# Delta-rule attention feeding a gated MLP: products of zeros that wait for the solve's steps, another order of the first chunk, weights held back, and the two correction products taken head by head

## The chip, the cores and the metric

The kernel runs on one core of a Trainium2 chip. The metric is the device time of one execution in microseconds (us), compared as the median of several executions.

## What is computed

```python
def _attn_ref(q, k, v, beta):                    # 4 x 8 heads, 768 steps, head size 48
    k_n = k / (np.linalg.norm(k, axis=-1, keepdims=True) + 1e-06)
    for t in range(S):
        kt, vt, bt = (k_n[:, :, t], v[:, :, t], beta[:, :, t, None])
        y[:, :, t] = np.einsum('bhd,bhde->bhe', q[:, :, t], state)
        v_old = np.einsum('bhde,bhd->bhe', state, kt)
        state = state + bt[:, :, :, None] * np.einsum('bhd,bhe->bhde', kt, vt - v_old)
...
def _moe_ref(x, w_in, w_out):                    # x is 3072 x 384, hidden 2048
    h = x @ w_in
    sp = np.where(h > 20.0, h, np.log1p(np.exp(np.minimum(h, 20.0))))
    g = h * np.tanh(sp)
    return (g @ w_out).astype(np.float32)
```

The attention's output, with its heads side by side, is the input x of the MLP. The weights arrive as 64-bit numbers.

## The kernel before

**Chunks.** The 768 steps are cut into 12 chunks of 64. Within a chunk the recurrence is a triangular system. Its matrix comes from the Gram products of the keys (`pg`), is solved on VectorE in a chain of short steps (`pr`, `gt`, lines 605 and 606), and is turned into a matrix T (`tt`) and its transpose (`tn`). Two chunks are solved together: group 0 is chunks 0 and 1, group 1 is chunks 2 and 3. A diagonal block has 32 rows. Groups 0 and 1 solve blocks of 16 rows and join them by two sets of small products, `ma` and `mb` (lines 650 and 661). Then the two 32-row blocks of a chunk are joined by two products for each pair of heads, `ta` (function `s_a`) and `tb` (`s_b`). After that come, for each half of the heads, `gq` (queries and state against keys), `pz` (Z~, the corrected values), `py` (the output) and `ps` (the new state), and `xt`, which turns the output into x.

**The MLP.** For each chunk `moe` runs 8 blocks of hidden units: 18 products `h` (line 960), the activation `e` and its split `g`, and 12 products `acc` (line 970). The product is made in two halves of precision, so each weight is split too.

**The weights.** They come in 28 parts, 12 of `w_in` (`ri`, 512 KB) and 16 of `w_out` (`ro`, 384 KB). `convert` takes each from 64-bit words to a high and a low half: a scaled copy on ScalarE, a clamp and a sign on GpSimd or VectorE, two joins on VectorE (line 399), and for the parts in `LO_PE` the low half by products on TensorE (`loi`, `loo`, lines 416 and 418). A part below number `FIRST` is issued without waiting for the one ahead of it; the others wait until the one ahead has landed, and from `FREE` on only every second one waits.

**The order.** All loads of weights, keys and values stand in SyncE's queue, in order. A planner (`Plan.run`) plays all operations through with assumed durations and priorities, and writes each engine's instructions down in the order that this gives. It also keeps count of TensorE's instructions: 448 are taken to be there at the start, and further ones come in packets of 256. Tiles in PSUM are rings: four of tag `ps`, so `gq` of chunk 0, which writes four, holds all of them until the masks of line 838 have read them. `warm` is products of zeros into a tile that nobody reads.

The first chunk's TensorE work has negative priorities, written by hand at the end of the kernel:

```python
    for h in range(2):
        turn_q(0, h, -90.4 + 0.1 * h, q0)
        issue(-89.5 + 0.1 * h, s_gq(0, h))
    issue(-90, s_a(0))
    issue(-89, s_b(0))
```

## Time and profile before

| | us |
|---|---|
| median of 3 executions (lowest, highest) | 646.77 (645.03, 647.28) |
| the profiled execution | 645.29 |
| span of its instructions | 643.4 |
| TensorE busy | 602.8 |
| VectorE busy | 452.3 |
| ScalarE busy | 277.8 |
| GpSimd busy | 143.2 |

The span runs from the first to the last instruction; 1.9 us of the execution lie around it. PE is TensorE's products, PEld its weight loads, DVE VectorE, ACT ScalarE, POOL GpSimd, SP SyncE and SPq its DMA queue. PEclk is the granted TensorE clock as a share of full speed: 1.00 is 2.4 GHz, 0.50 is 1.2 GHz. In the trace one 32-bit product is recorded as two MATMULs and two LDWEIGHTS, so `x32` is 16 products of the code.

### The profile page before, as it was taken

To read this page: it belongs to the slowest core of one execution; us is meant where nothing else is said; L and a number is where in the kernel's file an instruction comes from. 1 tells how busy PE (TensorE), PEld (TensorE's weight loads), DVE (VectorE), ACT (ScalarE), POOL (GpSimd) and SP (SyncE) were. 2 spreads that over 40 slices of the span, in tenths; PEclk is the share of its full clock that TensorE was granted. 3 is DMA by queue.
4 is the path that set the end of the run, shared out by engine and by line. 5 is a ranking of instruction groups with operands and counts; after the bars stand their busy time and mean duration, and the time that the engine had idled before them with its cause. 6 is when DMAs were issued, how large, how long until landed. Compare 5 with 4: busy or idle time off the path is not lost.

```text
span 643.4 us, 20696 instructions
## 1 busy us (share of the span) xinstructions
PE 602.8 (94%) x8928; PEld 558.7 (87%) x8928; DVE 452.3 (70%) x964; ACT 277.8 (43%) x601; POOL 143.2 (22%) x146
## 2 busy tenths in 40 slices
PE   7339998995999999999999999999999999999997
PEld 7126677895999999999999999999999999999997
DVE  2866887899366999578999578997689994622110
ACT  2515888540554332544333644225543336343331
POOL 5646789241103110103111004001031101000000
PEclk8856996997899999999999999999999999999999
DMA  7764775210324110442112252104141111110011
GB/s 109 233 163 102 206 183 128 51 25 2 53 39 65 38 32 9 74 64 39 40 38 47 34 90 41 30 16 70 19 64 38 39 37 15 26 27 1 1 25 25
DMA packets 156251, 37.61 MB, mean 58 GB/s; under 512 B 149504, under 2 KB 152576, under 8 KB 156160
## 3 DMA queue, kind: packets, MB, share of 16 engines
q1 hardware_dynamic: 151040, 35.80, 28.0%
q8 instruction: 70, 1.15, 0.7%
q10 hardware_dynamic: 5120, 0.49, 0.6%
q14 instruction: 21, 0.17, 0.1%
HBM read 31.56 MB, written 4.72 MB: 56 GB/s over the span
## 4 chain that ended last, share of the span: by engine, by line
PE 69%; DVE 18%; DMA 5%; issue 3%; SPq 2%; POOL 1%; ACT 1%; DVEq 0%; ACTq 0%; POOLq 0%
PE acc L970 26%; PE h L960 25%; DVE pr L605 4%; DVE gt L606 3%; PE py L680 3%; DMA ri<-in_moe_w_in_dram 2%; PE gq L680 2%; PE tb L680 2%; PE pz L680 2%; DVE g L977 2%; DMA ksrc<-in_k_dram 2%; SPq L301 2%; PE pg L483 1%; PE ta L680 1%; PE ps L680 1%
## 5 line engine op out<-in xcount | busy, mean ns | idle before, releaser
L970 PE MATMUL acc<-wo,g 128*128 128x384 f32 x1152 | 225.7, 345 | 0.5 <-DVE g L977 0.5
L960 PE MATMUL h<-x,wi 128*128 128x256 f32 x1728 | 224.1, 284 | 0.0
L960 PEld LDWEIGHTS h<-x,wi 128*128 128x128 f32 x1728 | 213.4, 188 | 4.6 <-DVE x L939 0.7
L970 PEld LDWEIGHTS acc<-wo,g 128*128 128x128 f32 x1152 | 201.1, 191 | 4.2 <-DVE g L977 1.7
L977 DVE TENSOR_TENSOR g<-e,g 128x512 fp32r<-128x512 f32 x96 | 71.9, 753 | 103.9 <-ACT g L976 103.4
L975 ACT ACTIVATE e<-h 128x512 f32<-128x512 f32 x96 | 57.4, 598 | 162.6 <-DVE g L977 89.1
L976 ACT CAST g<-e 128x512 fp32r<-128x512 f32 x96 | 59.5, 619 | 61.9 <-PE acc L970 60.6
L512 POOL TENSOR_TENSOR d<-at,lmask 32x512 f32<-32x512 f32 x20 | 27.0, 1351 | 130.3 <-DVE d L498 94.1
L606 DVE TENSOR_TENSOR gt<-gt,pr 128x84 f32<-128x84 f32 (+14 forms) x148 | 51.9, 351 | 5.1
L605 DVE TENSOR_TENSOR pr<-gt 128x84 f32<-128x84 f32 (+14 forms) x148 | 52.3, 353 | 3.8
L838 DVE TENSOR_TENSOR xx<-gq,amask 64x256 f32<-64x256 f32 x96 | 40.5, 422 | 2.0
L638 POOL COPY tt<-tt 32x512 f32<-32x512 f32 x24 | 17.1, 714 | 100.2 <-DVE tt L621 85.2
L783 POOL TENSOR_TENSOR vt<-vt,ne 128x384 f32<-128x384 f32 x22 | 20.1, 932 | 72.4 <-DMA vt<-in_v_dram 67.5
L831 DVE TENSOR_TENSOR vt<-vt,gq 64x192 f32<-64x192 f32 (+1 forms) x66 | 23.2, 352 | 15.9 <-PE gq L680 11.4
L699 ACT COPY xx<-pz 64x192 f32<-64x192 f32 x92 | 28.9, 314 | 11.4 <-PE pz L680 10.1
L904 DVE TENSOR_TENSOR xx<-xx,ps 48x192 f32<-48x192 f32 x80 | 28.2, 352 | 3.2 <-PE ps L680 1.8
L680 PE MATMUL gq<-xx,kt 64*64 64x112 f32 (+1 forms) x768 | 30.0, 261 | 0.0
L680 PEld LDWEIGHTS py<-xx 128*64 128x64 f32 x768 | 24.3, 138 | 6.1 <-issue 3.7
L791 DVE STREAM_TRANSPOSE xx<-qsrc 64x512 f32<-64x512 f32 x40 | 28.2, 706 | 1.2
L650 PE MATMUL ma<-tu,d 16*32 16x16 f32 x512 | 7.2, 202 | 22.8 <-DVE xx L838 15.4
L680 PE MATMUL pz<-vt,tt 64*64 64x48 f32 x768 | 27.6, 225 | 0.8 <-ACT tt L699 0.8
L650 PEld LDWEIGHTS ma<-tu,d 16*32 16x32 f32 x512 | 6.8, 139 | 24.1 <-issue 23.5
(143 smaller groups left out, 690.9 us busy)
## 6 DMA issues: line engine op xcount, KB each, us to landing
ri<-in_moe_w_in_dram SPq DMA_DIRECT2D x12, 512.0 KB, 4.6
ro<-in_moe_w_out_dram SPq DMA_DIRECT2D x16, 384.0 KB, 4.3
vt<-in_v_dram SPq DMA_DIRECT2D x24, 192.0 KB, 3.5
xx<-in_k_dram SPq DMA_DIRECT2D x48, 96.0 KB, 2.9
out_dram<-o SPq DMA_DIRECT2D x48, 96.0 KB, 2.2
ksrc<-in_k_dram SPq DMA_DIRECT2D x44, 64.0 KB, 2.6
qsrc<-in_q_dram SPq DMA_DIRECT2D x40, 64.0 KB, 2.5
ksrc<-in_k_dram SPq DMA_DIRECT2D x44, 32.0 KB, 2.5
```

Source lines behind the costliest of these rows:

```text
L605: nc.vector.tensor_tensor(out=pv, in0=nj, in1=xj, op=ALU.mult)
L606: nc.vector.tensor_tensor(out=below, in0=below, in1=pv, op=ALU.add)
L680: nc.tensor.matmul(*a, start=True, stop=True)
L699: (nc.scalar.copy if e == "ACT" else nc.vector.tensor_copy)(out=a, in_=b)
L791: nc.vector.transpose(xx[h][r, :, hh, D:D + C], src)
L838: nc.vector.tensor_tensor(out=x[r, p4, hh, D:D + C], in0=pg[h4]()[i, :, d:], in1=bcast_mid(amask[i], 4), op=ALU.mult)
L904: nc.vector.tensor_tensor(out=old, in0=old, in1=ps[h4]()[i], op=ALU.add)
L960: nc.tensor.matmul(h()[:, f2, :], wt["i", f * P // WI * NCH + c][:, i2, f0:f0 + P], x[:, c, :], start=(i == 0), stop=(i == 3 * NCH - 1))
L970: nc.tensor.matmul(acc[t]()[:, :DM], gg()[:, a, f2, ts_], wt["o", f][:, i2, :], start=(f == 0 and i == 0), stop=(f == NF - 1 and i == 2))
L975: m = op("ACT", 0.58, prio + 0.1, lambda e=e, h=h: nc.scalar.activation(e(), h(), AF.Mish, scale=-1.0), m, bufs=[h, e])
L976: m = op("ACT", 0.58, prio + 0.1, lambda e=e, gg=gg: nc.scalar.copy(out=gg()[:, 0], in_=e()), m, bufs=[e, gg])
L977: m = op("DVE", 0.7, prio + 0.1, lambda e=e, gg=gg: nc.vector.tensor_tensor(out=gg()[:, 1], in0=e(), in1=gg()[:, 0], op=ALU.subtract), m, ...
```

## The change

It has five parts. (1) The products of zeros at the start are 15 of 512 columns in place of 66 small ones. Those beside the solve no longer follow each other freely: `warm_after` puts four behind a step of the solve, and three behind the last join of the first ten weight parts, with a semaphore wait on that very instruction; the planner leaves out a group that it would place over 0.5 us after the step. (2) Both Grams of group 0 come ahead of the turning of the queries (`grams[1]` in `qread`), the queries' load waits for the first Gram, the values' load for the queries', and by the planner's order `gq` of chunk 0 now stands behind `mb`. (3) Nine weight parts instead of six are issued without waiting (`FIRST`), and the tenth waits for the product Z~ of chunk 0's first half of heads (`GATE`); those behind it are loaded one at a time up to the 26th (`FREE`). (4) From chunk 2 on `ta` and `tb` are products of one head, 32x32 each, over four places of the array; chunks 0 and 1 keep the old form as `s_a2` and `s_b2`. (5) The planner's model of instruction packets is different, small products next to each other get a slight preference (`TOGETHER`), four priorities move, the 25th part's low half goes to TensorE, and `py` of chunk 0 no longer waits for the keys that only `ps` reads.

```diff
-    THERE, PACKET, ASK, TAKES = 448, 256, 308, 2.6
+    THERE, PACKET, ASK, AHEAD, TAKES = 448, 256, 244, 64, 2.6
+    CHANGE, TOGETHER = 0.2, 0.0
...
-                    times = [(max(free[e], when(o)), o.prio, i, o) for i, o in enumerate(ops)]
+                    times = [(max(free[e], when(o)), o.prio - self.TOGETHER * (group and o.words >= 64), i, o)
+                             for i, o in enumerate(ops)]
...
+            if o.late is not None and t > o.after[0].free + o.late:
+                o.took, o.words, o.bufs, o.fn = 0.0, 0, [], lambda: None
...
+            if n == 0 and hh == 0:
+                tc.add_manual_dep(d.ins, gram_ins[0].name, SYNC, reason="instructions first")
...
-    def load_w(kind, i, paced):
+    def load_w(kind, i, paced, gate):
...
+        if gate:
+            tc.add_manual_dep(d.ins, marks[gate].name, SYNC, reason="instructions first")
...
+        if k < WARM:
+            warm_after(o, 3)
...
-            for i in range(few + n):
-                m = 32 if i < few else P
-                nc.tensor.matmul(warm()[0:m, 0:4 * m], zero()[:, 0:m], zero()[:, 0:4 * m], start=True, stop=True)
+            for i in range(n):
+                x = identr.bitcast(BF16) if after in marks else zero()[:, 0:512]
+                p = nc.tensor.matmul(warm()[:, :x.shape[1]], x[:, 0:P], x, start=True, stop=True)
+                if i == 0 and after in marks:
+                    tc.add_manual_dep(p.ins, marks[after].name, SYNC, reason="not before")
...
-    WARM = {2: 2, 8: 12}
-    keep_warm(0, o, -210, few=66)
+    marks, WARM = {}, 10
+    def warm_after(o, n):
+        f = o.fn
+        def marked():
+            marks[o] = f()
+        o.fn = marked
+        keep_warm(n, o, -85)
+    keep_warm(15, o, -210)
...
-            if g == 0 and j in WARM:
-                keep_warm(WARM[j], o, -96)
+            if g == 0 and j > 1:
+                warm_after(o, 4)
...
+    def halves():
+        return [PB * i + p for p in range(PB) for i in range(2)]
...
+    def s_a(n):
+        at, tt = ats[n], tt2[:, n % 2]
+        ps = buf("ps", [P, NP, 32], f"ta{n}")
+        def products():
+            for p in halves():
+                for hh in range(2):
+                    r = slice(64 * hh + 32, 64 * hh + 64)
+                    i = 64 * hh + 32 * (p // PB)
+                    yield ps()[i:i + 32, p, :], at()[r, p, :], tt[r, p, 32:]
...
+    def s_b(n):
...
+            for p in halves():
+                for hh in range(2):
+                    r = slice(64 * hh, 64 * hh + 32)
+                    i = 64 * hh + 32 * (p // PB)
+                    yield ps()[i:i + 32, p, :], tn()[r, n % 2, p, :], at()[r, p, :]
...
-        m = qread[n, h] = op("PE", 1.0, prio, products, *got, eyer, ydn.get((n - 1, h)), gdn.get((n - 1, h)), bufs=[ps], words=64)
+        m = qread[n, h] = op("PE", 1.0, prio, products, *got, eyer, grams[1], ydn.get((n - 1, h)), gdn.get((n - 1, h)), bufs=[ps], words=64)
...
-                     [*zdn[n, h], *ptr[n, h], *kxd[n, h], cleared_rest, *(() if y else (ydn[n, h],))],
+                     [*zdn[n, h], *ptr[n, h], *(kxd[n, h] if state else ()), cleared_rest, *(() if y else (ydn[n, h],))],
...
-    E1S, LAG, PRIO_XT, CV0, CV1, G1A, XA, GQ2 = 0.471, 3, 0.289, -0.48, 0.819, 1.125, 0.027, 0.985
-    LO_PE = range(24)
-    FIRST, FREE = 6, 13
+    E1S, LAG, PRIO_XT, CV0, CV1, G1A, XA, GQ2 = 0.471, 3, 0.354, -0.48, 0.919, 1.108, 0.027, 0.985
+    LO_PE = range(25)
+    FIRST, FREE = 9, 26
+    plan.TOGETHER = 0.019
+    GATE = 3
...
-    q0, v0 = load_q(0, -99.5), load_v(0, -99.4)
+    q0 = load_q(0, -99.5, grams[0])
+    last_s["v"] = q0
+    v0 = load_v(0, -99.4)
...
+    first = [issue(-90, s_a2(0)), issue(-89, s_b2(0))]
+    first += [issue(-88 + 0.1 * h, s_z(0, h)) for h in range(2)]
+    first += [issue(-87 + 0.1 * h, s_y(0, h, state=False)) for h in range(2)]
+    if GATE:
+        stop[0] = first[GATE - 1]
+        got[FIRST].after.append(stop[0])
```

Where the instructions go is shown at three places. The first is TensorE from the end of chunk 0's Gram to chunk 0's Z~, of the kernel before; `kt_194` and `kt_277` are the turned keys of chunks 0 and 1, and each line of one kind stands once for its run.

```order
L489 MATMUL pg_1_205<-kt_194 32x64 x4
L804 MATMUL qt_0_290<-identr,qsrc 48x64 x16
L804 MATMUL qt_1_307<-identr,qsrc 48x64 x16
L489 MATMUL pg_0_326<-kt_277 32x64 x4
L446 MATMUL warm<-zero 128x512
L680 MATMUL gq_00_477<-xx_80,kt_194 64x64 x2
L650 MATMUL ma_591<-tu_576,d_266 32x16 x64
L661 MATMUL mb_665<-tt_82,ym_281 32x16 x64
L416 MATMUL loi_743<-mi_429,identr 128x512
L680 MATMUL ta_748<-tt_82,at_267 64x64 x16
L418 MATMUL loi_743<-wi_745,identr 128x512
L680 MATMUL tb_775<-at_267,tn_733 64x64 x16
```

The same stretch of TensorE after the change, where `kt_223` is chunk 1's keys.

```order
L523 MATMUL pg_0_232<-kt_223 32x64 x4
L895 MATMUL qt_0_318<-identr,qsrc 48x64 x16
L895 MATMUL qt_1_339<-identr,qsrc 48x64 x16
L465 MATMUL warm<-identr 128x256
L684 MATMUL ma_496<-tu_491,d_214 32x16 x64
L695 MATMUL mb_571<-tt_82,ym_227 32x16 x64
L717 MATMUL gq_00_644<-xx_80,kt_143 64x64 x2
L717 MATMUL ta_666<-tt_82,at_215 64x64 x16
L436 MATMUL loi_686<-mi_384,identr 128x512
L717 MATMUL gq_10_692<-xx_81,kt_143 64x64 x2
L438 MATMUL loi_686<-wi_569,identr 128x512
L717 MATMUL tb_719<-at_215,tn_642 64x64 x16
```

Chunk 1's Gram now follows chunk 0's at once; `gq` has gone from ahead of `ma` to behind `mb`, its two halves on either side of `ta`; between the queries' turning and `ma` stand 16 products of zeros (four behind each of the steps 2 to 5 of the solve), and none behind the steps 6 to 14.

The second place is SyncE's queue from the first weight parts on. Before:

```order
L348 DMA ro_420<-in_moe_w_out_dram 128x768
L348 DMA ro_498<-in_moe_w_out_dram 128x768
L301 DMA xx_80<-in_k_dram 64x8x48 x2
L348 DMA ri_560<-in_moe_w_in_dram 128x1024
L301 DMA xx_81<-in_k_dram 64x8x48 x2
L348 DMA ri_582<-in_moe_w_in_dram 128x1024
L301 DMA vt_584<-in_v_dram 64x16x48 x2
L348 DMA ri_659<-in_moe_w_in_dram 128x1024
```

And after the change, where `ri_784` is the tenth part, the one that waits for Z~:

```order
L363 DMA ro_374<-in_moe_w_out_dram 128x768
L363 DMA ri_377<-in_moe_w_in_dram 128x1024
L363 DMA ri_380<-in_moe_w_in_dram 128x1024
L312 DMA qsrc<-in_q_dram 64x16x48 x2
L363 DMA ri_784<-in_moe_w_in_dram 128x1024
L312 DMA xx_80<-in_k_dram 64x8x48 x2
L363 DMA ro_848<-in_moe_w_out_dram 128x768
L312 DMA xx_81<-in_k_dram 64x8x48 x2
```

The eighth and ninth part moved ahead of the wait; chunk 0's keys for the state (`xx_80`, `xx_81`) and all that stands behind moved behind it.

The third place is TensorE in the steady part, `ta` and `tb` of chunks 2 and 3, whose middle ones are issued four and four. Before:

```order
L680 MATMUL ta_2560<-tt_82,at_1869 64x64 x16
L680 MATMUL tb_2604<-at_1869,tn_2485 64x64 x4
L680 MATMUL ta_2605<-tt_82,at_1907 64x64 x4
L680 MATMUL tb_2794<-at_1907,tn_2485 64x64 x16
```

And after:

```order
L717 MATMUL ta_2551<-tt_82,at_1863 32x32 x32
L717 MATMUL tb_2627<-at_1863,tn_2452 32x32 x4
L717 MATMUL ta_2628<-tt_82,at_1902 32x32 x4
L717 MATMUL tb_2846<-at_1902,tn_2452 32x32 x32
```

Each has twice as many products of half as many columns.

## Rows read from the trace of the kernel before

**Rows 1.** Busy time of each engine by stage, from the windows of the trace: start and end, length, then for PE, PEld, DVE, ACT and POOL busy us (instructions), then the granted clock, the share of the DMA engines and GB/s.

```profile
37.00:69.50 32.50, 25.35 (x510) 17.72 (x511) 21.30 (x41) 14.95 (x33) 16.70 (x12) 0.64 0.56 133
69.50:136.30 66.80, 64.39 (x1052) 52.73 (x1052) 56.15 (x98) 49.41 (x107) 47.45 (x34) 0.92 0.52 126
180.00:643.00 463.00, 458.62 (x6082) 438.67 (x6074) 323.40 (x704) 186.32 (x401) 48.44 (x52) 1.00 0.22 38
```

**Rows 2.** The same view cut where the granted clock changes (the column before the last two).

```profile
26.00:37.00 11.00, 0.00 (x0) 0.00 (x1) 10.16 (x26) 4.73 (x14) 9.63 (x7) 0.50 0.58 148
37.00:60.00 23.00, 16.75 (x392) 11.72 (x392) 12.01 (x25) 7.18 (x16) 13.43 (x10) 0.50 0.43 108
60.00:97.50 37.50, 35.65 (x611) 26.17 (x610) 32.78 (x55) 32.02 (x69) 26.36 (x19) 1.00 0.80 201
```

**Rows 3.** The timeline of the first 21 us: start, length, engine, line, operation, out<-in, count, and in brackets the idle time ahead with what ended it.

```profile
7.06 2.05 PE L489 MATMUL pg<-kt 64*32 64x64 f32 x128
8.18 1.25 DVE L467 STREAM_TRANSPOSE kt<-ksrc 128x1024 f32<-128x1024 f32 x1 [1.40 <-DMA ksrc<-in_k_dram]
...
11.55 2.95 PE L804 MATMUL qt<-identr,qsrc 64*48 64x64 f32 x62 [1.72 <-DMA qsrc<-in_q_dram]
...
14.43 2.60 PE L489 MATMUL pg<-kt 64*32 64x64 f32 x128
...
17.50 1.39 PE L680 MATMUL gq<-xx,kt 64*64 64x64 f32 x64
...
18.82 2.76 PE L446 MATMUL warm<-zero 128*128 128x512 bf16 x12
```

**Rows 4.** The timeline from the end of the solve to Z~ and to the first `h`, same columns.

```profile
33.33 1.07 DVE L619 STREAM_TRANSPOSE tu<-gt 128x512 f32<-128x512 f32 x1
...
36.05 3.48 DVE L838 TENSOR_TENSOR xx<-gq,amask 64x256 f32<-64x256 f32 x8
37.03 2.10 PE L650 MATMUL ma<-tu,d 16*32 16x16 f32 x128 [15.44 <-DVE xx L838]
...
43.15 1.78 PE L661 MATMUL mb<-tt,ym 32*32 32x16 f32 x115 [3.15 <-issue]
...
46.76 2.07 PE L416 MATMUL loi<-mi,identr 128*128 128x512 f32 x2 [1.83 <-DVE mi L399]
...
48.76 1.97 PE L680 MATMUL ta<-tt,at 32*64 32x64 f32 x32
...
50.66 0.80 PE L418 MATMUL loi<-wi,identr 128*128 128x512 f32 x1
...
53.09 1.97 PE L680 MATMUL tb<-at,tn 32*64 32x64 f32 x32
...
56.56 2.34 PE L680 MATMUL pz<-vt,tt 64*64 64x48 f32 x64 [0.77 <-ACT tt L699]
...
69.55 2.65 PE L960 MATMUL h<-x,wi 128*128 128x256 f32 x21
```

**Rows 5.** The profile's page: busy time and instructions of TensorE, and the queue that carries instructions (packets, MB, share of 16 engines); then, from its list of loads, the queries' load of chunks 0 and 1 (count, KB, us from issue to landing).

```profile
PE 602.8 (94%) x8928; PEld 558.7 (87%) x8928; DVE 452.3 (70%) x964; ACT 277.8 (43%) x601; POOL 143.2 (22%) x146
...
q8 instruction: 70, 1.15, 0.7%
...
qsrc<-in_q_dram SPq DMA_DIRECT2D x4, 192.0 KB, 3.5
```

**Rows 6.** The timeline of SyncE's queue, weight parts alone: from one row to the next is the interval of paced loads.

```profile
35.45 0.33 SPq L348 DMA_DIRECT2D ri<-in_moe_w_in_dram  x1
...
39.77 0.33 SPq L348 DMA_DIRECT2D ri<-in_moe_w_in_dram  x1
...
44.03 3.44 SPq L348 DMA_DIRECT2D ro<-in_moe_w_out_dram  x2
...
95.17 0.83 SPq L348 DMA_DIRECT2D ro<-in_moe_w_out_dram  x2
...
100.43 0.82 SPq L348 DMA_DIRECT2D ro<-in_moe_w_out_dram  x2
```

**Rows 7.** The timeline around the start of the second solve (line 526 turns its matrix).

```profile
126.34 0.56 DVE L399 SCALAR_TENSOR_TENSOR solved<-solved,ro 128x384 int32<-128x384 int32 x1 [1.10 <-POOL ro L392]
...
128.73 2.38 PE L960 MATMUL h<-x,wi 128*128 128x256 f32 x18
...
130.06 5.77 POOL L512 TENSOR_TENSOR d<-at,lmask 32x512 f32<-32x512 f32 x4 [3.75 <-ACT at L503]
...
136.30 2.06 DVE L526 STREAM_TRANSPOSE gt<-d 128x1024 f32<-128x1024 f32 x1
```

**Rows 8.** The timeline of small products at full clock: `mb` of chunk 1, and the first row of the `tb` and `ta` that are issued four and four, with the first row behind them.

```profile
94.27 1.26 PE L661 MATMUL mb<-tt,ym 32*32 32x16 f32 x128
...
267.21 0.27 PE L680 MATMUL tb<-at,tn 32*64 32x64 f32 x2
...
268.35 2.40 PE L960 MATMUL h<-x,wi 128*128 128x256 f32 x18
```

**Rows 9.** The chain of work that ended last, near the same place: start, us, what.

```profile
259.65 2.11 PE acc L970 x12
...
263.89 1.08 PE ta L680 x32
264.97 2.31 PE acc L970 x12
```

More of the change, by code (lines that the diff above doesn't have):

```diff
@@ L29, in __init__ @@
         self.bufs = bufs
-        self.next, self.left, self.free, self.kb, self.words, self.sync = [], 0, None, 0, 0, False
+        self.next, self.left, self.free, self.kb, self.words, self.sync, self.late = [], 0, None, 0, 0, False, None
 class Buf:
@@ L80, in feed @@
                 there, done = there + self.PACKET, None
-            if done is None and there <= self.ASK and left > 0:
+            if done is None and there <= self.ASK + min(self.AHEAD, left + 32) and left > 0:
                 done = t + self.TAKES + max(0.0, line - t)
@@ L95, in run @@
     def run(self):
-        there, due = self.THERE, None
+        there, due, group = self.THERE, None, False
         free, line, used, ready, flying = {}, 0.0, {}, {}, []
@@ L149, in run @@
                     used.setdefault(b.tag, []).append(b)
+            if o.words:
+                if group and o.words >= 64 and t < free[e] + 0.1:
+                    o.took -= self.CHANGE
+                group = o.words >= 64
             free[e] = t + o.took
@@ L679, in run_all @@
                 for a in f[i:i + 4]:
-                    nc.tensor.matmul(*a, start=True, stop=True)
+                    last = nc.tensor.matmul(*a, start=True, stop=True)
+        return last.ins
     class Stage:
@@ L688, in issue @@
     def issue(prio, *stages):
-        m = op("PE", sum(s.took for s in stages), prio, lambda: run_all(*(s.products() for s in stages)),
+        def products():
+            marks[m] = run_all(*(s.products() for s in stages))
+        m = op("PE", sum(s.took for s in stages), prio, products,
                *(a for s in stages for a in s.after), bufs=[b for s in stages for b in s.bufs], words=sum(s.words for s in stages))
```

63 lines of the change are left out of this document (43 added, 20 removed).

## The prediction

> **What bounds the kernel now.** I read the windows by stage first. From 180 us to the end TensorE is busy 458.6 of 463 us at full clock [rows 1]: that stretch ends sooner only if TensorE has less to do. The room lies ahead of it. Between 26 and 60 us the clock is 0.50, which is 1.2 GHz, and in the first 11 us of that TensorE does nothing [rows 2]; up to 136 us it is busy nearly throughout, with VectorE at 56.2 of 66.8 us [rows 1]. So I read the start as a chain in the timeline, link by link.
>
> Four waits stand in it. (a) Chunk 1's keys are turned at 9.43 us (8.18 + 1.25), but its Gram starts at 14.43, because the queries' turning stands ahead of it in TensorE's queue and waits for a load until 11.55 [rows 3]. (b) The solve's result `tu` is there at 34.40, but `ma` starts at 37.03. The four PSUM tiles are held by `gq` until the masks have read the first, and those are VectorE's next work, from 36.05 on [rows 4]. (c) `mb` stops after 13 recorded products for 3.15 us, with nothing that the profile can name [rows 4]. TensorE's 8928 products and 8928 loads over the 70 packets of the instruction queue make 255 a packet [rows 5]. Counted in the order, 1210 instructions lie ahead of the stop (products of zeros 132 + 4 + 24, Grams 2 x 256, turning 128, `gq` 128, `ma` 256, `mb` 26), and the plan's own constants make 448 + 3 x 256 = 1216. So I take it for a missing packet. (d) Chunk 0's stage from `ma` to `pz` runs at half clock [rows 2, 4].
>
> Then the weights: once `h` has begun at 69.55 [rows 4], the next fixed point is the second solve, whose matrix is turned at 136.30. Ahead of it, in VectorE's order, stands the join of the last weight part at 126.34; GpSimd's four products `d` end at 135.83 [rows 7].
>
> **The change, part by part.**
>
> *Grams first.* Chunk 1's Gram can start at 9.45 instead of 14.43: -5.0. What follows keeps its order. The queries' load is now issued after the first Gram's end at 9.11 [rows 3]; with 3.5 us to landing [rows 5] the queries are there at about 12.6, and ScalarE's copy of them, which stands ahead of the solve's root, ends as the root is wanted. If the load lands 2 us later, 2 us go: the bounds are -3.0 and -5.0.
>
> *`gq` behind `mb`.* No tile is held at `ma`: it starts 0.1 us after `tu`, -2.5. The masks move to VectorE's wait for `mb`, so they cost nothing until `ta`'s result wants VectorE.
>
> *The packet.* Up to `ma` there are now 30 + 256 + 256 + 128 + 32 = 702 instructions, and `ma` has 256. The boundary 960 falls at the head of `mb` again, but no weight load is under way then, where before a 512 KB part was issued at 39.77, inside the stop [rows 6]. I take -3.0; the bounds are 0 and -3.15.
>
> *Between `mb` and `tb`.* This takes 8.15 us now, from 44.94 to 53.09. Afterwards a half of `gq` (0.7 at full, 1.4 at half clock), `ta` (1.90), a `loi` (2.07), the other half, 0.72 and another `loi` (1.7) stand in a row: 9.2 at half clock, +1.0, or 4.9 at full, -3.2 [rows 3, 4]. The products of zeros don't decide it. They end behind step 5 of the solve, at about 22 us, some 7.5 us ahead of `ma`; in the trace the clock fell at 26.0, 4.4 us after the last such product at 21.58 [rows 2, 3]. So `ma` starts at half clock again. Afterwards TensorE has fewer gaps than now and may rise earlier. Between the ends I take 0.
>
> *From `tb` to `h`.* Six products of zeros stand ahead of `xt`, and each group waits for a join that VectorE does just then. They are 128x256, half of the 0.23 us that a 512-column one took [rows 3]: +0.3, with bounds 0 and +0.7. The 15 at the very start lie in TensorE's wait for the keys and cost nothing.
>
> Together: -5.0 - 2.5 - 3.0 + 0 + 0.3 = -10.2. `h` starts at 59.3, and the first half of Z~, now at about 57.7, ends at 47.2.
>
> *Weights held.* Seventeen parts go one at a time from 47.2 us on, then a pair. Alone, a 512 KB part took 4.3 us and a 384 KB part 3.1 (39.77 to 44.03, and the second of the next row); in the thick of the other loads a pair took 5.3 (95.17 to 100.43) [rows 6]. Seven large and ten small ones make 3.6 on average alone; 5.3 is the other end, if one costs what a pair costs. A pair also moves a second part, so I take 4.0, nearer to the lone rows. Then the 26th has landed at 115 and the last pair at 120.5, some 15 us later than now. With 3.5 us for copy, clamp and sign the last join stands at 124, only 2.3 us sooner than 126.34. Behind it come `d`, the copies and two of GpSimd's products (2.9 of the 5.77), so the matrix is turned at about 130.3 instead of 136.30 [rows 7]. TensorE gives the same: from `h` to the seventh `h` it takes 59.2 us now [rows 4, 7], one `acc` (2.2) comes ahead, a part's low half and three groups of zeros add 2.2, and 59.3 + 63.6 = 122.9 is 5.8 sooner. So 4.2 of the 10.2 are given back. The bounds are 0 and, at 5.3, far more than all of it (below).
>
> The second solve and the wait for it keep their length. What stands behind them on TensorE is the same `h` and `acc`.
>
> *Single heads.* A `ta` or `tb` by itself takes 1.08 us for 32 recorded products [rows 9]. `mb` of chunk 1 is the nearest row: 32x32 pieces over four places, 16 columns, 128 in 1.19 (1.26 less a tail), 9.3 ns apart [rows 8]. At that pace 64 take 0.6. The other end: `mb` holds a place 37 ns (4 x 9.3) for 16 columns; 16 more, at the 1.05 ns a column of `ta`'s two places now (67 ns for 64), make 54, and 16 of those in each place 0.86. I take 0.72, so -0.36 each, ten times: -3.6, with bounds 0 and -4.8. The five that are issued four and four now take 1.14 for 64 [rows 8]; 128 at 9.3 ns take 1.19, so nothing. The Trainium skill, "TensorEngine Tiling (Array Packing)", section Instruction Overhead, says that a product with few columns has the same latency as one of 60, and that a small dimension should not be cut further. By it the sum would be that of the last rival below.
>
> *Fewer changes.* An `acc` behind `ta` takes 2.31, behind `h` 2.11 [rows 9]. Counted in the order, TensorE goes from small to full products 57 times instead of 60 after the second solve: -0.6.
>
> **Sum.** The profiled execution took 645.29 us. 645.3 - 10.2 + 4.2 - 3.6 - 0.6 = 635.1. The median of the runs is 1.5 above that execution, so I forecast 636.5.
>
> **The rivals.**
>
> *The clock rises early.* TensorE works nearly without a gap from `ma` on and is at full clock from `mb`. Then -3.2 holds between `mb` and `tb`, and `mb`, `tb` and `pz` get some 2.5 to 3.3 shorter (`mb` 1.26 for 1.78, `tb` 1.08 for 1.97, `pz` about half of 2.34) [rows 4, 8, 9]. Z~ and the weights come 6.5 us sooner: 630. For it speaks that the clock rose at 60 us, 3.5 us after `pz` began [rows 2, 4]; against it, that it did not rise from 46.8 to 56 us, with `loi`, `ta` and `tb` in a row.
>
> *The weights come too late, and it is slower.* One paced part takes as long as a pair, 5.3. Then the 26th lands at 137.3, the last pair at 142.6, its join stands at 146 and the matrix is turned at 152.5, 16 us later than now: 645.3 + 16.2 - 4.2 + 1.5 = 659. It decides from 4.6 us a part on, where the loss equals the 4.2 of the steady part. For it speaks that keys, queries and values, which stand behind the wait, are loaded between the parts; against it, the lone 4.3 and 3.1.
>
> *The start is hidden anyway.* VectorE is busy 84% of 69.5 to 136.3 and cannot be pressed much, and at 4.35 us a part the second solve starts when it does now. Only the steady part is left: 645.3 - 4.2 + 1.5 = 642.6.
>
> *Single heads cost what two cost.* 34 ns a product, as `ta` now, makes 64 of them 2.16, +1.08 ten times, and the mixed ones double, +1.14 five times: +16.5 in place of -3.6, so 656.5. Against it stand the 9.3 ns of `mb`. The rule quoted above from the Trainium skill speaks for this one.
>
> **How the numbers follow.** I give the forecast 0.47 (its own range is 631 to 642), the early clock 0.18, the late weights 0.12, the hidden start 0.12, the dear single heads 0.04; 0.07 is left for what I don't see. 0.3% of the median, 1.9 us, is about what a measurement of this kernel can tell from no change. Faster by more: the first two, most of the hidden start and a little of the rest, 0.77; within it 0.08; slower 0.15, the late weights with the dear heads. The range goes from 627, below the early clock, to 646, which leaves out the two slow rivals.
>
> **What would show it.** Chunk 1's Gram should start near 9.5 us, `ma` near 29.5 without a wait for masks, `mb` without a stop; the tenth weight part is issued near 47, those behind it 4.0 us apart, the last landing near 120; the second solve's matrix is turned near 130; a lone `ta` takes about 0.7 us. The prediction is wrong if the clock in chunk 0's stage is full, if the parts stand over 4.6 us apart, or if TensorE waits at a product of zeros for a join that comes late.

## The result: slower by 0.6%, and the profile after

| | before | after |
|---|---|---|
| median of 6 executions, us | 646.74 (645.03 to 648.69) | 650.38 (649.78 to 651.24) |
| profiled execution, its span | 645.29, 643.4 | 650.02, 648.3 |
| after to before, 95% interval | | 1.0057 (1.0038 to 1.0077) |

Executions over 1.5% above the fastest of their kernel are left out of all medians and ratios here; that concerns two of e13, one of them its profiled one.

I had forecast 636.5. The start as a whole, up to the first `h`, came out within half a microsecond of the forecast, though not term by term; the time was lost behind it. The timeline of the changed kernel from the first Grams to the first `h` (answers to [rows 3, 4]):

```profile
7.53 3.37 PE L523 MATMUL pg<-kt 64*32 64x64 f32 x208
11.98 0.88 PE L523 MATMUL pg<-kt 64*32 64x64 f32 x48 [1.08 <-issue]
...
13.60 1.93 DVE L560 STREAM_TRANSPOSE gt<-d 128x1024 f32<-128x1024 f32 x1
...
14.92 3.65 PE L895 MATMUL qt<-identr,qsrc 64*48 64x64 f32 x62 [0.33 <-DMA qsrc<-in_q_dram]
...
17.82 0.35 DVE L596 RECIPROCAL rc<-y 128x32 f32<-128x32 f32 x1 [1.89 <-ACT y L580]
...
31.79 1.90 PE L684 MATMUL ma<-tu,d 16*32 16x16 f32 x127 [7.02 <-DVE tu L653]
35.44 0.18 PE L684 MATMUL ma<-tu,d 16*32 16x16 f32 x1 [1.76 <-issue]
36.09 1.90 PE L695 MATMUL mb<-tt,ym 32*32 32x16 f32 x127 [0.47 <-ACT ym L688]
39.27 0.23 PE L695 MATMUL mb<-tt,ym 32*32 32x16 f32 x1 [1.27 <-issue]
...
47.88 1.27 PE L717 MATMUL tb<-at,tn 32*64 32x64 f32 x32
...
49.66 2.32 PE L717 MATMUL pz<-vt,tt 64*64 64x48 f32 x64
...
59.75 2.40 PE L1051 MATMUL h<-x,wi 128*128 128x256 f32 x18
```

`ma` starts 5.2 us sooner than before and `h` 9.8 sooner (59.75 against 69.55). The wait for masks is gone, but there are three short stops "issue", and the solve waits 1.89 us for ScalarE.

Then SyncE's weight parts, the end of the conversions, and the start of the second solve (answers to [rows 6, 7]):

```profile
51.60 0.33 SPq L363 DMA_DIRECT2D ri<-in_moe_w_in_dram  x1
55.77 0.33 SPq L363 DMA_DIRECT2D ro<-in_moe_w_out_dram  x1
...
118.94 6.09 SPq L363 DMA_DIRECT2D ro<-in_moe_w_out_dram  x3
```

```profile
128.01 0.36 DVE L412 TENSOR_SCALAR solved<-solved 128x384 f32<-128x384 f32 x1 [3.58 <-ACT solved L401]
...
133.62 0.56 DVE L416 SCALAR_TENSOR_TENSOR solved<-solved,ro 128x384 int32<-128x384 int32 x1
...
138.74 2.98 POOL L546 TENSOR_TENSOR d<-at,lmask 32x512 f32<-32x512 f32 x2 [1.76 <-ACT at L537]
...
141.99 2.03 DVE L560 STREAM_TRANSPOSE gt<-d 128x1024 f32<-128x1024 f32 x1
...
161.36 2.21 PE L684 MATMUL ma<-tu,d 16*32 16x16 f32 x148 [11.65 <-DVE tu L653]
```

The tenth part is issued at 51.60 (before at 39.77), the 26th at 118.94, and the last pair at 124.22 (before at 100.43). VectorE waits 3.58 us for a part of the weights, the last join begins at 133.62 instead of 126.34, and the matrix is turned at 141.99 instead of 136.30. So 15.5 us (9.8 + 5.7) are lost between `h` and the second solve. TensorE then waits 11.65 us for the solve, where it waited 6.19 before. Busy times by stage (columns as in [rows 1]):

```profile
69.50:136.30 66.80, 59.81 (x894) 47.22 (x894) 44.50 (x81) 41.37 (x89) 40.65 (x31) 0.92 0.61 139
...
180.00:647.90 467.90, 460.31 (x6802) 441.73 (x6800) 324.13 (x704) 192.71 (x412) 48.28 (x52) 1.00 0.22 38
```

In the stretch in which VectorE was to be the bound it has 11.7 us less to do than before, and TensorE is busy 59.81 us instead of 64.39. Both wait mostly for weights: 14.9 us of VectorE's idle time there and 5.5 of TensorE's end with a step of their conversion (the view of waits).

### The profile page after: what moved, and what is told of

Same layout as the page of the kernel before. It is cut to its first block, busy times and chain, and to the rows that moved or that the text cites. A ratio compares the mean times of both kernels' runs of the same rounds, so it can differ in the third digit from the quotient of the medians.

```text
span 648.3 us, 21898 instructions
## 1 busy us (share of the span) xinstructions
PE 601.7 (93%) x9531; PEld 552.7 (85%) x9531; DVE 451.1 (70%) x963; ACT 279.0 (43%) x602; POOL 141.8 (22%) x146
## 3 DMA queue, kind: packets, MB, share of 16 engines
q8 instruction: 75, 1.23, 0.8%
## 4 chain that ended last, share of the span: by engine, by line
PE 58%; DVE 25%; issue 6%; DMA 5%; ACT 2%; POOL 2%; SPq 1%; DVEq 0%; POOLq 0%; ACTq 0%
PE acc L1061 22%; PE h L1051 20%; DVE pr L639 5%; DVE gt L640 5%; DMA ro<-in_moe_w_out_dram 2%; DVE xx L929 2%; PE gq L717 2%; PE py L717 2%; DMA ri<-in_moe_w_in_dram 2%; DVE gt L560 2%; PE tb L717 1%; PE pg L517 1%; DVE g L1068 1%; DVE vt L922 1%; PE ta L717 1%
## 5 line engine op out<-in xcount | busy, mean ns | idle before, releaser
L1061 PE MATMUL acc<-wo,g 128*128 128x384 f32 x1152 | 222.3, 343 | 0.0
L640 DVE TENSOR_TENSOR gt<-gt,pr 128x84 f32<-128x84 f32 (+14 forms) x148 | 53.7, 363 | 5.1
L874 POOL TENSOR_TENSOR vt<-vt,ne 128x384 f32<-128x384 f32 x22 | 19.8, 922 | 66.9 <-DMA vt<-in_v_dram 62.1
L717 PE MATMUL gq<-xx,kt 64*64 64x112 f32 (+1 forms) x768 | 32.0, 275 | 0.0
L922 DVE TENSOR_TENSOR vt<-vt,gq 64x192 f32<-64x192 f32 (+1 forms) x66 | 23.3, 352 | 10.6 <-PE gq L717 9.4
L717 PEld LDWEIGHTS pz<-vt,tt 64*64 64x64 f32 x768 | 23.0, 133 | 5.7 <-issue 2.8
L684 PE MATMUL ma<-tu,d 16*32 16x16 f32 x512 | 7.5, 202 | 21.7 <-DVE tu L653 18.7
```

Of the source, the lines that this page charges most:

```text
L640: return nc.vector.tensor_tensor(out=below, in0=below, in1=pv, op=ALU.add).ins
L717: last = nc.tensor.matmul(*a, start=True, stop=True)
L922: nc.vector.tensor_tensor(out=vt()[r, p4, :], in0=vt()[r, p4, :], in1=pg[h4]()[i, :, 0:D], op=ALU.subtract)
L1061: nc.tensor.matmul(acc[t]()[:, :DM], gg()[:, a, f2, ts_], wt["o", f][:, i2, :], start=(f == 0 and i == 0), stop=(f == NF - 1 and i == 2))
```

## The experiments

All spans can be split in three: TensorE's work at full clock (busy time times granted clock, summed over windows of 2 us), what half clock adds to its busy time, and its idle time. "Gram behind" is the work that TensorE's order puts ahead of the Gram of chunks 2 and 3 (products of `h`/`acc`; two entries where its halves are apart), "matrix" the time at which the second solve's matrix is turned. The ratio is to the kernel before on the same chip; the runs stand on three chips, on which its median was 646.2 to 647.4.

| kernel | median us | ratio (95%) | Gram behind | matrix | work / half clock / idle |
|---|---|---|---|---|---|
| before | 646.7 | | 108/24 | 136.30 | 583.7 / 19.1 / 40.6 |
| after | 650.38 | 1.0057 (1.0038 to 1.0077) | 108/48 | 141.99 | 583.7 / 18.0 / 46.6 |
| e1 old loading | 648.78 | 1.0025 (1.0003 to 1.0047) | 108/36, 126/48 | 138.74 | 582.0 / 12.1 / 50.2 |
| e2 not held | 640.92 | 0.9899 (0.9873 to 0.9925) | 90/24, 108/24 | 129.97 | 583.8 / 13.6 / 41.5 |
| e3 held, pairs | 647.71 | 1.0008 (0.9986 to 1.0030) | 90/24 | 135.46 | 583.3 / 19.8 / 43.2 |
| e4 xt as before | 644.77 | 0.9960 (0.9936 to 0.9984) | 108/48, 126/60 | 139.61 | 581.5 / 17.0 / 43.9 |
| e5 e2, xt as before | 640.56 | 0.9908 (0.9889 to 0.9926) | 90/24, 108/24 | 132.27 | 583.4 / 18.7 / 38.6 |
| e6 e2, two heads | 640.95 | 0.9912 (0.9886 to 0.9937) | 90/24, 108/24 | 128.19 | 587.8 / 13.3 / 38.1 |
| e7 e2, no zeros | 639.66 | 0.9890 (0.9870 to 0.9910) | 90/24 | 127.13 | 579.7 / 13.8 / 44.4 |
| e8 e2, order as before | 642.06 | 0.9926 (0.9907 to 0.9944) | 108/24, 108/36 | 128.61 | 585.1 / 12.9 / 42.4 |
| e9 e2, pairs | 639.30 | 0.9873 (0.9843 to 0.9904) | 108/24 | 130.19 | 582.6 / 18.7 / 38.0 |
| e10 e2, six free | 644.25 | 0.9955 (0.9936 to 0.9975) | 108/24 | 128.17 | 584.3 / 14.6 / 43.5 |
| e11 before, nine free, single | 656.84 | 1.0151 (1.0126 to 1.0176) | 72/12, 144/72 | 150.92 | 585.0 / 21.1 / 48.5 |
| e12 e5, no zeros | 637.51 | 0.9856 (0.9832 to 0.9880) | 90/24 | 126.79 | 580.8 / 14.1 / 40.9 |
| e13 after's order, wait out | 647.29 | 0.9994 (0.9967 to 1.0022) | 108/48 | | |
| e14 held, Gram early | 649.90 | 1.0048 (1.0029 to 1.0066) | 72/12 | 134.33 | 585.4 / 17.2 / 47.4 |
| e15 before, six free, single | 648.47 | 1.0024 (1.0008 to 1.0041) | 90/12, 126/36 | 139.31 | 588.5 / 11.3 / 45.1 |
| e16 e12, pairs | 642.40 | 0.9920 (0.9894 to 0.9946) | 108/24 | 135.51 | 579.6 / 18.7 / 42.5 |
| e17 e2, six parts doubled | 652.22 | 1.0078 (1.0053 to 1.0104) | 90/24, 108/24 | 142.40 | 583.6 / 17.6 / 50.0 |
| e18 e12, queries early | 641.09 | 0.9890 (0.9854 to 0.9926) | 90/24 | 134.10 | 580.3 / 17.4 / 42.2 |

### The hold, the single parts, the number of free parts

e2, and all that are told as "not held", is the changed kernel with this edit alone:

```diff
-    GATE = 3
+    GATE = 0
```

e1 has it too, and the two sizes of before; e3 keeps `GATE = 3` and has `FIRST, FREE = 9, 13`:

```diff
-    FIRST, FREE = 9, 26
+    FIRST, FREE = 6, 13
```

e1. 

> The changed kernel with the loading of before: the wait for Z~ taken out, six parts free, then single parts up to the 13th, then pairs. Theory A (the weights come too late for the second solve): the last part lands near 105 us again, the joins end near 123 or sooner, h still starts near 60, and the second solve's matrix is turned at 130 to 134 instead of 142: 639 to 643 us. Theory B (the start is hidden whatever the loading: VectorE and TensorE have no less to do up to the second solve): the matrix is turned at 138 to 142 and the time is 647 to 651. Theory C (the held loads are what brought Z~ forward): h starts at 63 or later, mb's stop is longer, and half or less of the 8 us is got back: 645 to 648.

e2. 

> The changed kernel without the wait for Z~, but nine parts free and then one part at a time up to the 27th. It tells the hold from the single parts. Theory A with the hold as the cause: the tenth part is issued near 22 us, seventeen more at 4.4 us end near 97, and the matrix is turned at 130 to 134: 639 to 643 us, like the old loading. Theory A with the single parts as the cause: the matrix comes at 137 or later, 646 or more. Theory B: 647 to 651.

e3. 

> The changed kernel with the wait for Z~ kept, but in pairs from the 14th part on (as before) instead of one at a time up to the 27th. Theory A with the single parts as the cause: 51.6 us, four single parts of 4.4 and eight pairs of 5.3 end near 111 instead of 128, the last join near 122, and the matrix is turned near 131: 639 to 642 us. Theory A with the hold as the cause: the conversions start too late all the same, the waits of TensorE for low halves between 85 and 100 us stay, the matrix is turned at 136 or later: 645 or more. Theory B: 647 to 651.

Measured, by the medians: e2 takes back all of the loss and 6 us more; e3 takes 2.7 and e1 1.6, which the intervals can't tell from nothing. With single parts the hold costs 9.5 us (after against e2), with pairs 8.4 (e3 against e9, below). So the hold, with the order that the plan makes of it, is the cause, and the single parts are a small part of the loss: theory A, with the hold. e1 has no hold and yet stays outside theory A's 639 to 643. The rows of e2 for the tenth and the last parts, the second solve, and the two stretches:

```profile
30.46 0.33 SPq L363 DMA_DIRECT2D ri<-in_moe_w_in_dram  x1
...
92.59 8.29 SPq L363 DMA_DIRECT2D ro<-in_moe_w_out_dram  x4
```

```profile
129.97 2.06 DVE L560 STREAM_TRANSPOSE gt<-d 128x1024 f32<-128x1024 f32 x1
```

```profile
28.00:37.00 9.00, 3.83 (x182) 3.47 (x185) 8.76 (x12) 3.33 (x6) 8.39 (x6) 0.50 0.61 138
69.50:136.30 66.80, 63.83 (x981) 52.88 (x980) 51.08 (x98) 45.53 (x98) 38.60 (x30) 0.99 0.50 104
```

The parts come 20 to 25 us sooner, VectorE has 6.6 us more to do up to 136 us, and the matrix is turned 12.0 us sooner. That Z~ now comes later (`pz` at 55.88 instead of 49.66) and `h` at 75 costs nothing. e9 and e10 ask what e1 lost by its two sizes: e9 is e2 with `FIRST, FREE = 9, 13`, e10 is e2 with `FIRST, FREE = 6, 26`.

e9. 

> The kernel that doesn't hold the weights, with pairs from the 14th part on (nine free as in the changed kernel). The old loading not held took 648.8 us and nine free with single parts 640.9: this tells which of the two sizes makes the 8 us. Theory P (pairs bring the conversions onto VectorE and ScalarE while chunk 0's stage needs them): 646 to 649, with the wait of 6 us for yy ahead of xt and a wait of ma for a part. Theory Q (it is six free instead of nine): 640 to 642.5.

e10. 

> The other half of the pair: not held, six parts free, then one at a time up to the 27th. Theory P: 640 to 643. Theory Q: 646 to 649. If both this and the run before stand near 641, neither size alone makes the loss of the old loading, and it lies in the order that goes with both.

Pairs with nine free parts cost nothing (639.30 against 640.92), six free with single parts cost 3.3 us, and both together 7.9. So theory P is refuted, and theory Q holds only in part. In e10 the second solve starts as early as in e2 and the loss lies behind 180 us (11.9 us idle against 6.9); in e1 the order puts 18 `h` and 12 `acc` between the halves of the Gram, where e2 has 18 `h` alone, and 18 `h` and 12 `acc` more ahead of the first. I take these for losses of the order that the plan makes; no run here shows it.

### Late data, or the order that goes with the hold?

Taking the hold out also moved the Gram forward by two groups of `acc` (48 products to 24, some 4.3 us), and its first half by a group of `h` more.

e13 leaves the plan as it is and takes out only the wait, e14 moves the Gram with the hold kept, and e17 is e2 with parts loaded twice. Their edits, in this order:

```diff
-                    lambda kind=kind, i=i, k=k: load_w(kind, i, PACED(k), stop[0] if k == FIRST else None),
+                    lambda kind=kind, i=i, k=k: load_w(kind, i, PACED(k), None),
```

```diff
-    SOON, SOON1, E1, EG, ES, LATE1, LATE = -0.058, 0.925, 0.521, -0.785, 1.433, 0.174, 0.334
+    SOON, SOON1, E1, EG, ES, LATE1, LATE = -0.058, 0.925, 0.42, -0.785, 1.433, 0.174, 0.334
```

```diff
         d = nc.sync.dma_start(out=r, in_=src)
+        if 9 <= len(came) < 15:
+            d = nc.sync.dma_start(out=r, in_=src)
```

e13. 

> The changed kernel with every instruction of every engine in its place; only the tenth part's wait for Z~ is taken out. It tells the late weights from the order that the plan makes when it reckons with the hold. Theory L (late data): the parts land 15 us or more sooner, TensorE's 7 us of waits for low halves between 60 and 140 us go, and the second solve's matrix is turned at 134 to 137 instead of 142: 643 to 646 us. Theory O (the order: two more groups of acc stand ahead of the third and fourth chunk's Gram, 48 products instead of 24): the matrix is turned at 139 to 142, 648 to 651.

e14. 

> The changed kernel with the hold kept and one number of the order changed (the place of the next Gram, 0.42 for 0.521): the Gram stands behind 72 products of h and 12 of acc instead of 108 and 48. Theory O: the second solve's matrix is turned 8 us sooner or more, at 134 or before, and the time is 642 to 646. Theory L: the conversions of the late weights stand ahead of it on VectorE all the same and TensorE waits for low halves behind it: 648 to 652.

e17. 

> The kernel that doesn't hold the weights, with the 10th to 15th part each loaded twice, one copy behind the other into the same place: every instruction of the computing engines stands where it stood, only the data (and the loads that stand behind them in SP's queue) come later, the last part issued near 118 us instead of 93, as late as in the changed kernel. Theory L (late weights are what the hold costs): the second solve's matrix is turned at 138 to 145 instead of 130, the granted clock falls towards 0.955, the time is 647 to 653. Theory O (the order that goes with the hold costs it): less than 3 us is lost, 641 to 644.

e13 didn't do what I meant. Its queue, up to the 13th part:

```profile
28.98 0.33 SPq L363 DMA_DIRECT2D ri<-in_moe_w_in_dram  x1
...
36.26 0.33 SPq L363 DMA_DIRECT2D ro<-in_moe_w_out_dram  x1
36.63 17.54 SPq L312 DMA_DIRECT2D vt<-in_v_dram  x4
54.22 0.74 SPq L363 DMA_DIRECT2D ro<-in_moe_w_out_dram  x1
```

Three parts came early; the fourth stands behind loads of values that wait 17.5 us for chunk 0's stage, and the last pair is issued at 124.92, no sooner than with the wait (124.22). So the order that the plan makes with the hold keeps the queue back even without the wait, and this run separates nothing. Its 647.29 us lie 3.1 below the changed kernel, between the two theories.

e14 decides for neither. Its matrix is turned 7.7 us sooner, near where theory O had it, but the time is theory L's. TensorE waits for `x`, which VectorE makes at 146.03, behind the first steps of the solve:

```profile
146.56 3.99 PE L1051 MATMUL h<-x,wi 128*128 128x256 f32 x17 [8.67 <-DVE x L1030]
```

From the turned matrix to the end e14 takes 515.7 us, the changed kernel 506.3. So an early matrix alone is worth nothing here.

e17 shows what late data alone do. The computing engines have exactly the order of e2; six parts are loaded twice, and what follows in the queue (weights, keys, queries and values) is later, the last parts by some 13 us:

```profile
58.83 0.82 PE L467 MATMUL warm<-identr 128*128 128x256 bf16 x3 [7.28 <-DVE spare L418]
```

```profile
105.75 7.21 SPq L363 DMA_DIRECT2D ro<-in_moe_w_out_dram  x4
```

```profile
142.40 2.07 DVE L562 STREAM_TRANSPOSE gt<-d 128x1024 f32<-128x1024 f32 x1 [1.20 <-POOL d L548]
```

The last four parts start 13.2 us later (105.75 against 92.59), the matrix is turned 12.4 us later, and the time is 11.3 us longer. From the turned matrix to the end both kernels take 508.9 us, so the delay passes on to the end as it is. The last parts were issued sooner than I had written (105.75, not 118), and the loss is as large all the same. But 5.4 of the 12.4 us arise ahead of the first `h` (80.50 against 75.13): TensorE stands 7.28 us at a product of zeros that waits for a join (3.54 us in e2). The prediction had named such a wait for a sign that it fails; the changed kernel has none there. The other 7.1 us arise between `h` and the matrix, as in the changed kernel.

What held up the changed kernel's own second solve, its trace says. The view of the chain that ended last (start, us, what; the view infers who released whom) passes from Z~ into the tenth part, and at its end from landing to landing, through the last conversions to the matrix:

```profile
51.60 4.11 DMA ri<-in_moe_w_in_dram
55.77 3.17 DMA ro<-in_moe_w_out_dram
...
108.98 6.56 DMA ri<-in_moe_w_in_dram
115.60 3.32 DMA ro<-in_moe_w_out_dram
118.94 5.22 DMA ro<-in_moe_w_out_dram
124.22 3.19 DMA ro<-in_moe_w_out_dram
127.44 0.55 ACT solved L401
...
134.21 1.62 DVE solved L416
...
142.06 1.97 DVE gt L560
```

In e2 the chain leaves the weights when the last of them has landed, at 103.1, and comes to the matrix through TensorE's products, the Gram among them:

```profile
99.41 3.69 DMA ro<-in_moe_w_out_dram
...
121.59 1.09 PE pg L517 x64
122.68 2.31 PE acc L1061 x12
...
130.05 1.99 DVE gt L560
```

So by this view late weights set the time of the changed kernel's matrix, and e17 shows that late data with the order kept cost 7.1 us on that same stretch. How much of the lateness is the wait, how much the queue's order (in the chain the 24th part, at 108.98, stands behind loads of keys that wait until 106.4 for the keys' buffers), and what the order costs besides, no run tells.

### The kernel before with single parts

The edit of e11 in the kernel before; e15 has `6, 26` instead:

```diff
-    FIRST, FREE = 6, 13
+    FIRST, FREE = 9, 26
```

e11. 

> The kernel before with one edit: nine parts free and then one at a time up to the 27th (no hold, nothing else of the change). Theory R (single parts make the gain of the kernel that isn't held, and the rest of the change next to nothing): 641 to 643.5 us. Theory S (the gain is that of the Grams first and gq behind mb, which the hold had hidden): 645.5 to 648.

e15. 

> The kernel before with single parts from the seventh to the 27th, six free as before; the Gram of chunks 2 and 3 stays near its place (behind 90 and 126 products of h, before 108), where the run with nine free had moved it to 72 and 144. If single parts by themselves cost or gain nothing, 645.5 to 648; if they make the loss of the run with nine free, 652 or more; if they are a gain that the moved Gram had hidden, below 644.

Neither theory of e11 had a loss of 9.5 us in it. There the plan puts the second half of the Gram behind 144 `h` and 72 `acc`, and the matrix is turned at 150.92. With the Gram near its place (e15) single parts cost 1.6 us. I take the Gram's place for the cause of e11's loss; only these two runs speak for it. So e11 says nothing of the pace, and of the gain of e2 over the kernel before neither run tells how much the Grams first make.

### Where the gain of the single heads went

e4 puts `PRIO_XT` back to 0.289 in the changed kernel, e5 does so in e2. e6 is e2 with the old form of `ta` and `tb` everywhere, e8 is e2 with all four numbers of the order as before. The edits of e6 and e8:

```diff
-                issue(u + G1A + late, s_a(n + 1))
-                issue(u + G1A + 0.1 + late, s_b(n + 1), s_a(n + 2))
-                issue(u + G1A + 0.3 + late, s_b(n + 2))
+                issue(u + G1A + late, s_a2(n + 1))
+                issue(u + G1A + 0.1 + late, s_b2(n + 1), s_a2(n + 2))
+                issue(u + G1A + 0.3 + late, s_b2(n + 2))
```

```diff
-    E1S, LAG, PRIO_XT, CV0, CV1, G1A, XA, GQ2 = 0.471, 3, 0.354, -0.48, 0.919, 1.108, 0.027, 0.985
+    E1S, LAG, PRIO_XT, CV0, CV1, G1A, XA, GQ2 = 0.471, 3, 0.289, -0.48, 0.819, 1.125, 0.027, 0.985
...
-    plan.TOGETHER = 0.019
+    plan.TOGETHER = 0.0
```

e4. 

> The changed kernel with one number of the order put back: the priority of xt (0.354 again 0.289). It asks where the 4 us of the single heads went. Theory D (the later place of xt is what makes TensorE wait 0.9 us for x once in a pair of chunks, from 180 us on): these waits go, TensorE's idle time from 176 us to the end falls from 7.7 to about 4.4 us, and the time is 646.5 to 648. Theory E (they come with the shorter ta and tb, whose results VectorE cannot serve sooner): the waits stay or turn up elsewhere, 649.5 to 651.

e5. 

> The kernel that doesn't hold the weights, with the priority of xt of before as well. Theory D (the later xt makes the waits for x from 180 us on): the 2.6 us of them go nearly all, idle time of TensorE behind 180 us falls from 6.9 to about 4.5 us, 638 to 639 us. Theory E (the waits come with the short ta and tb): 640.5 to 642.

e6. 

> The kernel that doesn't hold the weights, with ta and tb of two heads everywhere as before. It prices the single heads. As forecast (0.36 saved for each lone one, nothing for the interleaved): TensorE's work counted at full clock rises by 3.6 to 4 us from 583.8 to about 587.6, and the time is 644 to 645. If the saving is eaten by waits for xt that the shorter products bring, the idle time behind 180 us falls by as much as the work rises: 640.5 to 642. If single heads cost more than two, it is faster: below 640.

e8. 

> The kernel that doesn't hold the weights, with all four numbers of the order as before: priority of xt, the step of the conversions' priorities, the place of ta and tb, and no bonus for full products together. If the bonus and the other three are worth the 0.6 us that I gave them, beside the xt that costs 2: 639 to 640. If the order made by these numbers is worth more: 642 or above; if it costs more than xt alone: 637.5 or below.

In the changed kernel a lone `ta`, and the engine that `xt` waits for (the view of all instructions on `xt`; us, times):

```profile
178.32 0.75 PE L717 MATMUL ta<-tt,at 32*32 32x32 f32 x64
```

```profile
  DVE x L1030: 3.2, 4
```

The product is as cheap as forecast: 0.68 us to the next instruction. e6 confirms it with two heads: TensorE's work rises by 4.0 us, from 583.8 to 587.8. But the time is the same, because its idle time falls. Behind 180 us, e2 and then e6:

```profile
180.00:638.50 458.50, 451.97 (x6568) 433.43 (x6567) 322.71 (x703) 186.46 (x398) 48.17 (x52) 1.00 0.22 38
```

```profile
180.00:638.80 458.80, 454.77 (x6020) 434.60 (x6018) 320.93 (x701) 185.45 (x396) 46.99 (x52) 1.00 0.22 38
```

6.5 us of idle time become 4.0. In e2 the wait of `xt` for `x` is 2.2 us (3 times); in e6 there is none. So most of the saving turns into idle time, 2.2 us of it waits for VectorE (theory E), and what is left is lost in the scatter. With the old priority of `xt` these waits go too (e5: none), and 0.4 us is all that comes of it, not a difference that the intervals can tell; in e4 more came (5.6, below both its theories), but there the Gram and all around it had moved. With all four numbers as before (e8) the time is 1.1 us longer, which the intervals can't tell from nothing: the 0.6 us for fewer changes are neither shown nor excluded.

### The zeros and the start

e7 takes the zeros behind the solve's steps and the joins out of e2, and e12, below, out of e5. e18 is e12 without the wait of the queries' load for the first Gram. Their edits:

```diff
-        keep_warm(n, o, -85)
```

```diff
-                tc.add_manual_dep(d.ins, gram_ins[0].name, SYNC, reason="instructions first")
+                pass
...
-    q0 = load_q(0, -99.5, grams[0])
+    q0 = load_q(0, -99.5)
```

e7. 

> The kernel that doesn't hold the weights, without the products of zeros behind the solve's steps and behind the first joins; the 15 at the very start stay. Theory F (they change nothing of the clock where it counts and cost what they take): the clock in 26 to 60 us stays within 0.05 of 0.70, the time is 639.5 to 641. Theory G (they keep the clock up in chunk 0's stage): the clock of that stretch falls to about 0.5 as in the kernel before, 4 us or more of chunk 0's stage come back, 643.5 to 646.

e18. 

> The fastest so far (not held, the priority of xt of before, no zeros behind the solve's steps; 637.5) with the queries' load back in its place at the start, no longer behind the first Gram. It prices the step 'Grams first': in the changed kernel the solve's root waited 1.9 us for ScalarE, which copied the queries that had come at 14.9 us. If the load was the cause, the wait goes, the solve's result comes 1 to 2 us sooner and the time is 636 to 637; if the Grams wait for their instructions instead (more loads beside them), the result comes no sooner and the time is 637 to 639.

In e7 the granted clock between 26 and 60 us is 0.71, with the zeros 0.70:

```profile
26.00:60.00 34.00, 25.07 (x510) 16.58 (x511) 31.79 (x56) 16.58 (x36) 28.36 (x21) 0.71 0.67 156
```

They change nothing there and take 4.1 us of TensorE's work, most of it in waits: the medians differ by 1.3 us, and the intervals overlap. Theory F. In e18 the Gram stops longer than in e12 (1.67 us for 1.23), and the matrix of the first solve is turned at 14.72 instead of 14.15 in e12:

```profile
12.58 1.50 PE L522 MATMUL pg<-kt 64*32 64x64 f32 x48 [1.67 <-issue]
```

The result comes 1.5 us later than in e12 (31.04 against 29.50). So for the start, holding the queries' load back was right, as the second expectation had it. Of the 3.6 us between the medians this explains only a part: the intervals overlap, and the order changed as well.

### The fastest

e12. 

> Not held, the priority of xt of before, and no products of zeros but the 15 at the start: the three edits that looked best, together. If they add up (0.4 and 1.3 us from 640.9): 638.5 to 639.5. If the zeros' 4 us of work lie beside waits all the same, 640 to 641.

e16 (e12 with `FIRST, FREE = 9, 13`). 

> Not held, nine free, pairs from the 14th part on, the priority of xt of before, no products of zeros but the 15 at the start. Pairs took 1.6 us less than single parts where nothing else differed; if that adds to 637.5, 635.5 to 637; if it was the scatter of the runs, 637 to 638.5; with a piece of the order going wrong, above 640.

e12 beats both kernels: 637.51 us, 1.4% below the kernel before and 2.0% below the changed one, and below both its expectations. Its matrix is turned at 126.79. It has the lowest median, but the intervals of e7 and e9 overlap with its own. Pairs don't add to it (e16): the same edit that gained nothing in e9 costs 4.9 us here, with the Gram behind one more group of `h` and the matrix at 135.51.

## Why the prediction was wrong

**Grams first (-5.0): 2.9 us.** Chunk 1's Gram starts at 9.6, as forecast. I had said that the copy of the queries "ends as the root is wanted". It doesn't: the Gram stops 1.08 us, the queries are there at 14.92 instead of 12.6, their turning follows, ScalarE copies before it makes the guess, and VectorE waits 1.89 us. The solve's first step is 2.9 us sooner, just short of my lower bound.

***gq* behind *mb* (-2.5): right.** `ma` starts 5.2 us sooner, 2.8 of them from the solve.

**The packet (-3.0): nothing.** I took the part that was issued inside the old stop for its cause. Now hardly any load is under way (columns as in [rows 1]):

```profile
30.50:39.50 9.00, 4.21 (x260) 3.81 (x263) 6.29 (x7) 2.22 (x4) 7.51 (x5) 0.50 0.04 8
...
48.00:60.00 12.00, 11.58 (x219) 8.52 (x220) 9.63 (x21) 8.38 (x20) 2.81 (x2) 0.99 0.45 114
```

and `ma` and `mb` stop for 1.76 and 1.27 us, 3.03 together against 3.15. In e2, with the DMA engines at 0.61, `ma` stops 1.66. The step that failed is that a quiet DMA ends the stop.

**Between *mb* and *tb* (0): +0.2. From *tb* to *h* (+0.3): -4.6.** The granted clock is 0.99 from 48 us on (second row above), where before it rose at 60 [rows 2]. This is a part of my rival "the clock rises early", and it made up for the two terms that failed: 59.75 for 59.3 is luck, the right number for partly wrong reasons.

**Weights held (+4.2): +15.5.** This is the step that failed. Of the 14.9 us between the 635.1 that my sum gives for the profiled execution and its 650.02 it makes 11.3; the steady part makes 3.4. Four things were mis-sized. Z~'s first half ended, and the tenth part was issued, at 51.60 instead of 47.2 (4.4 us). The parts stood 4.21 us apart, not 4.0, which over 16 intervals is 3.4. The rest of the way to the last join, which I had put at 124 and which stands at 133.62, is the last pair's landing and the copy, clamp and sign behind it, 1.8 us more than reckoned. From the last join to the turned matrix I had taken 6.3 us; [rows 7] give 7.1 (9.96 less 2.9), and it took 8.4. My rival "the weights come too late" named the mechanism, but I priced it by the pace alone ("It decides from 4.6 us a part on"). At a pace of 4.21 it was slower all the same, because the hold's own start and the way behind the last landing add to it. One more group of `acc` than I had counted stood ahead of the Gram too, but the chain above passes the joins, not the Gram. Worse, an early `h` was not what decided. In e2 `h` starts at 75, later than before, and the kernel is 6 us faster.

**"What stands behind them on TensorE is the same *h* and *acc*."** The work was the same (583.7 in both), the waits weren't. From the second `ma` to the end it took 487.7 us before and 486.9 after, 0.8 less instead of 4.2.

**Single heads (-3.6): the size was right (4.0 by e6), the place wrong.** I read 99% busy behind 180 us [rows 1] as a stretch that ends sooner with every product less. But work taken from TensorE at a place where `x` is not ready turns into a wait. The rival by which a lone `ta` takes 2.16 us failed: it took 0.68, 10.6 ns a product instead of 34. I had called the Trainium skill, "TensorEngine Tiling (Array Packing)", section Instruction Overhead, for it. The trace doesn't speak against what that section says: with four places taken in turn, one place has a product every 42 ns at 32 columns and every 37 at 16 (`mb`), so fewer columns saved little there. What failed was my price, which had the products one behind the other.

## To carry to other kernels

A load is held back safely only if what it feeds has slack: find the next point that everything waits for (here a second solve) and follow the data to it, through every conversion, before a chain that starts earlier is shortened. The view of the chain that ended last shows whether that data came last. Where a planner writes the order, a wait put into the plan moves instructions on all engines and other loads in the same queue. Then the wait taken out with the order kept can tell little (here the queue's order still held the loads), and the data made late with the order kept (loading it twice) tells more, once it is clear where its delay arises.

## What the runs showed of the hardware

TensorE makes short stops that the profile calls "issue" even when the DMA engines are nearly idle (share 0.04). I take them for waits for instructions by counting; the profile doesn't name their cause. In the changed kernel 446, 956 and 1212 recorded instructions lie ahead of the three stops (zeros 30, Grams 512, turning 128, zeros 32, `ma` 256; the Gram stops after 208 products, `ma` and `mb` after 127): the distances are 510, two packets of 255 [rows 5], and 256. `ma` and `mb` run through 254 instructions in 1.9 us each, and go on 3.65 us after `ma`'s start and 3.83 us after that, 0.47 of it a wait for `ym`. The Trainium skill, "Runtime: NRT & Kernel Launch", section Instruction fetch mechanics, says that fetching is hidden because instructions are issued more slowly than they are filled in. If the stops are what I take them for, the trace doesn't agree for these small products, at 7.5 ns an instruction (1.90 us by 254).

The mean granted clock of all executions is 0.950 in the changed kernel and 0.966 in e2; it is 0.950 to 0.960 in the five kernels whose plan has the hold (after, e3, e4, e13, e14) and 0.958 to 0.972 in the twelve others made from the changed one. The half clock adds 18.0 us to the changed kernel's profiled execution and 13.6 to that of e2, beside 5.1 us less idle time; of the 9.4 us between these two spans the clock is nearly half. But half clock doesn't go with the hold alone: e5 and e9, without it, have 18.7 us in their profiled executions and are no slower than e2 by more than the intervals can tell.
